# Moving a 64-byte scratch tile: attention's weights at another address beside the pages of h

## The chip, the cores and the metric

The program runs on one core of one Trainium2 chip. The metric is the device time in microseconds, the median of three runs: 2238.1 us (2237.97 to 2238.53). Beside it stands one profiled execution, from which every duration below is taken.

## The reference, cut to what matters

One transformer block over x of 2048 rows by 1024 columns. Six modulation vectors come from a small vector c; then attention with a linear memory, in 32 heads of 32 and 4 segments of 512 rows; then a mixer MLP across the rows.

```python
mod = (_silu(c) @ w_mod).reshape(c.shape[0], 6, 1, -1)
sa, ca, ga, sb, cb, gb = (mod[:, i] for i in range(6))
h = _layernorm(x) * (1 + ca) + sa
q, k, v = h @ wq, h @ wk, h @ wv          # 32 heads, 4 segments of 512
...
p = _softmax(q_s @ k_s.T * scale + mask)
o = g * (phi(q_s) @ M / den) + (1 - g) * (p @ v_s)
M = M + phi(k_s).T @ v_s
...
x = x + ga * (o @ wo)
h = _layernorm(x) * (1 + cb) + sb
x = x + gb * mixer(h, w1, b1, w2, b2)     # gelu MLP over the rows
```

## The kernel before, in words

**Numbers in two parts.** Large products are made in fp32r from operands split in two: a high part, and the rest. `split` (lines 118 to 125) writes both into one tile `[128, 2, 512]`, 4096 bytes in each partition, and each product takes three matmuls: high by high, high by rest, rest by high.

**Pages and weights.** The normed and modulated x, turned over, is `h`. It stays in SBUF in 16 "pages" of 4096 bytes (`new_page`, line 144), one for each segment and each 128 of the 1024 columns. For a group of four heads the projection weights stay in six of eight tiles tagged `w`, also 4096 bytes each (lines 156 to 171): four for k and v, two for q.

**The projections.** For each group (8) and segment (4), `project` calls:

- `kv_chunk` (line 188): the stationary operand, the one that is loaded into TensorE's array, is 128 columns of an h page; the moving operand, the one that streams through it, is 256 columns of a weight tile. This is line 195, output `nps`, 3072 matmuls in all.
- `q_chunk` (line 199): the other way round. The stationary operand is 128 columns of a weight tile, the moving operand a whole half page of h, 512 columns. This is line 203, output `qps`, 768 matmuls.

Every matmul has its own weight load, and all the steps from one operand slice to the next within these tiles are multiples of 512 bytes.

**The order of the work.** The program is written out in one stream. The main loop (line 691) steps through 128 pairs of head group, segment and head; in each step it issues `scores` of a head that comes three steps later in `maxima`, `values` of the head before, a quarter of a later `project`, and a list of extra jobs (`plan`, `later`) that were given a step by hand: token tiles, weight fetches, late modulation. A scheduler then orders each engine's instructions; on TensorE the projections' matmuls and those of scores and values alternate in short runs. After the loop come the output projection with `wo` (line 793, output `po`) and the MLP (line 923, output `mx`).

**Where things lie.** Tiles are given out from pools that stack up from the low end of each partition; each tile's size is rounded up to 32 bytes. From the low end:

- `const`: a few small tiles, among them `sc` and, opened late in the text at line 570, `mcol` (128 bytes);
- `page`: the 16 pages of h;
- `par`: five tiles of 4096 bytes (`scb`, `gaw`, three buffers `raw`);
- `acst`: `pad2` 32 bytes, `bd` 544, `csb` 64, `saca` 64, `MZ` 4224, `bdg` 4224: 9152 bytes in all;
- `paw`: the eight weight tiles `w`;
- above them the first stage's x and later `prj`, `late` and `sk`, with the operands of scores (`sk`, whose queries and keys are halves of one tile), values (`vp`) and memory (`pq`, `pk`, `v32`).

From the high end come `ident`, `mask` and, in the main loop, the softmax's `p32` and `ph`.

**Distance.** Pages and weights are multiples of 4096 apart, but for `acst`. 9152 is 35 times 256 plus 192, so each slice of a weight tile lies 192 bytes above a slice of a page, modulo 256; seen from the weights, the pages lie 64 above. In the output projection the pages hold `wo`, and the other operand `ots` lies above them with only tiles of 4096 and 8192 bytes between: a distance of 0. In the MLP the addresses of `sp` and of `bA`, `bB` and `bU` give 0 too. "Distance" below is always the address of the stationary operand less that of the moving one, modulo 256: 64 for line 195, 192 for line 203, 0 for lines 793 and 923.

**The two small tiles.** `csb` (line 104) takes the vector c at the start; the norms of the first two segments (`norm_all`, line 214, lines 217 to 236) then use its 16 floats as scratch for means, variances and scales. `mcol` takes the 32 sums of late modulation (`mod_late`, line 577), one column each, in the main loop.

Of the kernel before, what the change touches and what calls it, by code (L numbers as in the profile page):

```python
# [7 lines left out]
F32 = mybir.dt.float32  # L8
# [10 lines left out]
P = 128  # L19
NSEG, L = 4, 512  # L20
NK = D // P
# [23 lines left out]
def attention_and_mlp(ctx, tc, x, wq, wkv, wo, beta, w1, b1, w2, b2, c, wm_a, wm_b, out):  # L45
# [15 lines left out]
    const = ctx.enter_context(tc.tile_pool(name="const", bufs=1))  # L61
# [3 lines left out]
    a = par.__enter__()  # L65
    scb, gaw = (a.tile([P, D], F32, name=n) for n in ("scb", "gaw"))
    acst_pool = tc.tile_pool(name="acst", bufs=1)
    acst = acst_pool.__enter__()
# [32 lines left out]
    V.reciprocal(gate[:, 0], gate[:, 1])  # L101
    V.tensor_scalar(gate[:, 1], gate[:, 0], -1.0, 1.0, op0=ALU.mult, op1=ALU.add)

    csb = acst.tile([P, 2, NK], F32, name="csb")
    SY.dma_start(csb[:, 0], c)
    A.activation(csb[:, 1], csb[:, 0], AF.Exp, scale=-1.0)
    V.tensor_scalar_add(csb[:, 1], csb[:, 1], 1.0)
# [429 lines left out]
    def values(t, h):  # L537
# [28 lines left out]
        A.copy(ot, ps)  # L566
        SY.dma_start(oT[g, :, L * seg:L * seg + L], ot)
        del st[t]

    mcol = const.tile([P, 4 * NK], F32, name="mcol")  # L570

    def mod_fetch(j):
        r = a.tile([P, D], F32, tag="raw", bufs=3, name=f"rawm{j}")
# [569 lines left out]
```

## Time and profile before

| what | us |
|---|---|
| median of three runs | 2238.1 |
| the profiled execution | 2237.2 |
| its span | 2235.5 |
| outside the span | 1.7 |
| TensorE busy in the span | 2194.0 |
| VectorE, ScalarE, GpSimd busy | 1678.2, 1136.2, 731.9 |

A profile's row names an engine, a line and the program's tiles (out<-in). PE is TensorE's matmul, PEld its weight load. The mean of a group is the time of one matmul from start to end, pipeline included, so that matmuls overlap. What a matmul costs in a stream is the step from one start to the next, its pace. The view that shows it is the chain of work that ended last: a piece there gives its start, its length and the number of matmuls in a row, and length by number is the pace.

### The profile page before, as it was taken

What the parts mean: (1) busy time and instruction counts of PE and PEld (TensorE: products, weight loads), DVE (VectorE), ACT (ScalarE), POOL (GpSimd) and SP (SyncE); (2) the same over time, 40 slices, a digit from 0 to 9 for tenths busy, and PEclk for the clock granted to TensorE, in tenths of its full rate; (3) what the DMA queues carried; (4) which work ended last, traced back from release to release, by engine and by line L of the source; (5) the groups of instructions that cost most, each with busy time, mean ns of one, the idle gap of its engine ahead of it and who ended that gap; (6) DMA issues with size and microseconds to landing.
All of it is one profiled execution on the core that took longest, in us unless ns stands there. A gap on an engine that the chain in (4) does not pass through costs nothing.

```text
span 2235.5 us, 38277 instructions
## 1 busy us (share of the span) xinstructions
PE 2194.0 (98%) x13786; PEld 1883.5 (84%) x13786; DVE 1678.2 (75%) x3762; ACT 1136.2 (51%) x2082; POOL 731.9 (33%) x831
## 2 busy tenths in 40 slices
PE   8999999998999999999999999999999999999999
PEld 5989898887999899888888888888888888888887
DVE  7677677766777777655758766888888886969687
ACT  5477777665666666655546633533334242424232
POOL 2176666656777676654001200033330000000000
PEclk9999999999999999999999999999999999999999
DMA  7656665687566566665664587655556541414134
GB/s 284 192 175 205 170 180 168 179 299 230 163 194 194 162 197 185 195 192 181 226 205 161 222 328 261 251 212 222 206 201 232 204 144 59 153 57 146 57 123 151
DMA packets 175185, 423.05 MB, mean 189 GB/s; under 512 B 17524, under 2 KB 71828, under 8 KB 166036
## 3 DMA queue, kind: packets, MB, share of 16 engines
q1 hardware_dynamic: 174996, 420.61, 57.2%
q8 instruction: 109, 1.79, 0.3%
q14 instruction: 80, 0.66, 0.1%
HBM read 244.62 MB, written 125.06 MB: 165 GB/s over the span
## 4 chain that ended last, share of the span: by engine, by line
PE 84%; POOL 4%; DMA 3%; ACT 3%; DVE 3%; issue 2%; SPq 1%; ACTq 0%; DVEq 0%; POOLq 0%
PE mx L923 48%; PE nps L195 11%; PE po L793 8%; PE qps L203 6%; PE pv L549 3%; POOL ph L535 2%; PE a L520 1%; PE sz L484 1%; ACT ph L533 1%; DMA sk<-nt 1%; PE sx L484 1%; DVE wv L125 1%; POOL p L531 1%; PE a L523 1%; PE up L466 1%
## 5 line engine op out<-in xcount | busy, mean ns | idle before, releaser
L923 PE MATMUL mx<-bU,sp 128*128 128x512 f32 x2352 | 534.2, 389 | 0.9 <-DVE ac L930 0.9
L923 PEld LDWEIGHTS mx<-bU,sp 128*128 128x128 f32 x2352 | 441.1, 188 | 93.5 <-issue 1.3
L195 PE MATMUL nps<-wv,h 128*128 128x256 f32 x3072 | 437.9, 282 | 1.8 <-POOL h L125 0.7
L535 POOL TENSOR_TENSOR ph<-p,ph 128x640 f16<-128x640 f32 x256 | 383.6, 1520 | 156.1 <-ACT ph L533 153.3
L122 ACT CAST sp<-wr 128x384 fp32r<-128x384 f32 (+2 forms) x408 | 217.0, 545 | 426.7 <-PE mx L923 347.3
L923 PE MATMUL mx<-bA,sp 128*128 128x512 f32 x1764 | 430.5, 389 | 0.0
L195 PEld LDWEIGHTS nps<-wv,h 128*128 128x128 f32 x3072 | 404.6, 189 | 9.9 <-DVE h L125 2.0
L923 PEld LDWEIGHTS mx<-bA,sp 128*128 128x128 f32 x1764 | 331.1, 188 | 68.8
L125 DVE TENSOR_TENSOR sp<-wr,sp 128x384 fp32r<-128x384 f32 (+2 forms) x408 | 260.5, 650 | 31.1 <-ACT sp L122 30.8
L930 DVE TENSOR_TENSOR ac<-mx,ac 128x512 f32<-128x512 f32 x280 | 190.3, 688 | 85.1 <-PE mx L923 84.4
L203 PE MATMUL qps<-h,wq 128*128 128x512 f32 x768 | 198.3, 399 | 0.2
L533 ACT CAST ph<-p 128x1280 f16<-128x1280 f32 x128 | 161.3, 1260 | 44.4 <-POOL p L531 43.7
L793 PE MATMUL po<-wo,ots 128*128 128x512 f32 x768 | 179.3, 390 | 0.0
L793 PEld LDWEIGHTS po<-wo,ots 128*128 128x128 f32 x768 | 143.3, 188 | 29.0 <-DVE x L796 0.2
L923 PE MATMUL mx<-bB,sp 128*128 128x512 f32 x588 | 164.0, 389 | 0.0
L203 PEld LDWEIGHTS qps<-h,wq 128*128 128x128 f32 x768 | 140.7, 189 | 27.5 <-ACT vp L407 0.9
L531 POOL TENSOR_SCALAR_AFFINE_SELECT p<-p 128x256 f32<-128x256 f32 x256 | 121.9, 487 | 99.2 <-ACT p L528 52.4
L549 PE MATMUL pv<-vp,ph 128*128 128x97 bf16 (+1 forms) x2560 | 143.8, 203 | 3.0 <-DVE red L556 1.5
L549 PEld LDWEIGHTS <-ph 128*128 128x128 f16 x2560 | 115.8, 99 | 26.6 <-issue 11.5
L486 DVE CUSTOM_DVE_ANT_0 sx<-sx,mask 128x128 f32<-128x128 f32 (+1 forms) x256 | 93.8, 366 | 49.3 <-PE sx L484 47.4
L923 PEld LDWEIGHTS mx<-bB,sp 128*128 128x128 f32 x588 | 110.3, 188 | 22.9
L930 DVE TENSOR_TENSOR cc<-mx,cc 128x512 f32<-128x512 f32 x140 | 95.0, 685 | 39.6 <-PE mx L923 39.6
(207 smaller groups left out, 3165.7 us busy)
## 6 DMA issues: line engine op xcount, KB each, us to landing
sk<-sg SPq DMA_DIRECT2D x384, 128.0 KB
wr<-in_w_dram SPq DMA_DIRECT2D x28, 1024.0 KB
wr<-in_w_dram SPq DMA_DIRECT2D x32, 768.0 KB
bstu<-ucd SPq DMA_DIRECT2D x28, 768.0 KB
wsp<-wv SPq DMA_DIRECT2D x32, 512.0 KB
rawm<-in_wm_b_dram SPq DMA_DIRECT2D x32, 512.0 KB
wv<-wsp SPq DMA_DIRECT2D x32, 512.0 KB
pcd<-cc SPq DMA_DIRECT2D x14, 1024.0 KB
```

What stands on the lines that cost most here:

```text
L122: last_hi[0] = A.copy(hi, src)
L125: return lo_eng.tensor_tensor(lo, src, hi.bitcast(F32), op=ALU.subtract)
L195: T.matmul(ps[:, aa], h[:, j, 128 * tt:128 * tt + 128], wt[:, i, o:o + 256], start=(n == 0), stop=(n >= 6 * NK - 2), skip_group_check=True)
L203: T.matmul(ps, wt[:, i, o:o + 128], h[:, j], start=(k + n == 0), stop=(3 * k + n == 3 * NK - 1))
L486: marks[4 * t + h - LEADS, "V"] = V.tensor_tensor_reduce(o, o, mask[:, 384 - 128 * i:], 1.0, -3.0e38, op0=ALU.add, op1=ALU.max, accum_out= ...
L531: G.affine_select(w, w, pattern=[[0, 2], [1, 128]], compare_op=ALU.is_ge, fill=0.0, base=0, channel_multiplier=-1)
L533: marks[n, "A"] = A.copy(ph[:, 0], p32)
L535: marks[n, "G"] = G.tensor_tensor(ph[:, 1, c], p32[:, c], ph[:, 0, c], op=ALU.subtract)
L549: T.matmul(pv[:, i, 0:w], ph[:, part, o:o + 128], d["vp"][:, j, h, 0:w], start=(n == 0), stop=(n == 19), skip_group_check=True)
L793: T.matmul(ps, os_[:, i, P * ct:P * ct + P], wop[ct, nh][:, j], start=(n == 0), stop=(n == 3 * NK - 1))
L923: T.matmul(ps, ops[q][:, i, P * k:P * k + P], b[:, j], start=(m == 0 and first), stop=(m == 3 * nk - 1), skip_group_check=True)
L930: V.tensor_tensor(d, ps, d, op=ALU.add)
```

## The change

`mcol` is opened in `const` at the place where `csb` was made, and `csb` becomes a view of `mcol`'s first 16 columns. Nothing else is edited: no instruction is added, removed or changed in shape.

```diff
-    csb = acst.tile([P, 2, NK], F32, name="csb")
+    mcol = const.tile([P, 4 * NK], F32, name="mcol")
+    csb = mcol[:, 0:2 * NK].rearrange("p (a k) -> p a k", a=2)
     SY.dma_start(csb[:, 0], c)
     A.activation(csb[:, 1], csb[:, 0], AF.Exp, scale=-1.0)
     V.tensor_scalar_add(csb[:, 1], csb[:, 1], 1.0)
...
         SY.dma_start(oT[g, :, L * seg:L * seg + L], ot)
         del st[t]
 
-    mcol = const.tile([P, 4 * NK], F32, name="mcol")
-
     def mod_fetch(j):
```

In `const` only the order of the small tiles changes, not their sum, so the pages stay where they were. `acst` shrinks by 64 bytes to 9088, which is 35 times 256 plus 128. What lies above `csb` moves down by 64: `saca`, `MZ`, `bdg`, the weight tiles, and all of `prj`, `late` and `sk`. The distance is then 128 for line 195 and for line 203 alike.

## The prediction

> **What bounds the kernel now.** I read the page first: its span, the busy shares and the chain that ended last.
>
> ```profile
> span 2235.5 us, 38277 instructions
> PE 2194.0 (98%) x13786; PEld 1883.5 (84%) x13786; DVE 1678.2 (75%) x3762; ACT 1136.2 (51%) x2082; POOL 731.9 (33%) x831
> PE mx L923 48%; PE nps L195 11%; PE po L793 8%; PE qps L203 6%; PE pv L549 3%; POOL ph L535 2%; PE a L520 1%; PE sz L484 1%; ACT ph L533 1%; DMA sk<-nt 1%; PE sx L484 1%; DVE wv L125 1%; POOL p L531 1%; PE a L523 1%; PE up L466 1%
> ```
>
> TensorE is busy almost throughout, and four of its lines hold 73% of the chain. The change touches two, lines 195 and 203, 17% together. The view of busy time by windows says where they run: start, attention, output projection, MLP.
>
> ```profile
> 0.00:70.00 70.00, 60.35 (x353) 42.25 (x354) 50.72 (x105) 36.56 (x64) 17.71 (x52) 0.98 0.78 285
> 70.00:968.00 898.00, 870.85 (x7683) 796.92 (x7682) 646.69 (x1895) 592.44 (x1088) 571.65 (x665) 0.99 0.65 192
> 968.00:1160.00 192.00, 191.98 (x1035) 158.81 (x1034) 119.59 (x320) 93.63 (x169) 43.04 (x50) 1.00 0.62 207
> 1160.00:2235.50 1075.50, 1070.87 (x4722) 885.55 (x4720) 861.21 (x1445) 413.55 (x765) 99.51 (x64) 1.00 0.50 178
> ```
>
> The columns are window, length, busy time of PE, PEld, DVE, ACT and POOL, granted clock, DMA share and GB/s. In attention PE is busy 870.85 of 898 us, the next engine (DVE) 646.69; the granted clock is 0.98 to 1.00 everywhere, so a difference in pace between lines is not the clock's. Attention is the stage to read, and in it what one matmul costs.
>
> For that I use the chain in order of time: start, length, count. First the two lines that do not change, whose operands lie at distance 0.
>
> ```profile
> 1051.74 112.25 PE po L793 x495
> 1163.99 36.04 PE mx L923 x159
> ```
>
> 112.25 / 495 = 226.8 ns and 36.04 / 159 = 226.7 ns for 512 moving columns, over hundreds in a row. Half of it, 113.4, is what 256 columns would take at this rate. Now the two lines of the change, at distance 64 (nps, 256 columns) and 192 (qps, 512 columns).
>
> ```profile
> 61.64 8.04 PE nps L195 x68
> 76.87 2.96 PE nps L195 x26
> 199.53 2.50 PE nps L195 x22
> 206.79 2.47 PE nps L195 x21
> 225.61 2.06 PE nps L195 x18
> 477.54 3.53 PE nps L195 x31
> 481.83 3.17 PE nps L195 x27
> 500.67 2.52 PE nps L195 x22
> 710.79 2.29 PE nps L195 x20
> 187.09 5.51 PE qps L203 x24
> 727.65 4.83 PE qps L203 x21
> ```
>
> nps has two paces. Runs such as x26 (113.8), x22 at 199.53 (113.6) and x31 (113.9) sit on the floor of 113.4; others such as x68 (118.2), x21 (117.6) and x27 (117.4) are 4 ns above it. Over the nine rows it is 29.54 us / 255 = 115.8 ns. qps is on its floor in neither row: 10.34 / 45 = 229.8 ns against 226.8. The durations say the same of all matmuls (minimum, median, maximum of each line):
>
> ```profile
> L195 PE MATMUL nps<-wv,h x3072: 276/279/507, 26.4 to 958.6; 128*128 128x256 f32 x192
> L203 PE MATMUL qps<-h,wq x768: 387/393/689, 27.0 to 967.3; 128*128 128x512 f32 x192
> L793 PE MATMUL po<-wo,ots x768: 387/389/481, 968.3 to 1163.6; 128*128 128x512 f32 x192
> ```
>
> qps and po have the same shape and the same three products, yet their medians are 393 and 389 ns. So there is something to gain, and it is small: two lines, a few ns each.
>
> **The change part by part.** *The move of csb.* Its instructions stay. The question is a wait: `mod_late` will write into columns that the norms have read.
>
> ```profile
> L236 ACT ACTIVATE x<-x,csb x4: 1227/1258/1291, 18.0 to 49.5; 128x1024 f32<-128x1024 f32 x4
> L578 DVE SCALAR_TENSOR_TENSOR rawm<-rawm,scb x32: 1208/1624/2402, 397.9 to 862.6; 128x1024 f32<-128x1024 f32 x32
> ```
>
> The last reader of csb starts at 49.5 us and takes 1.3; the first writer of mcol starts at 397.9. A wait, if one is written, has been over for 347 us. It costs nothing; were the cover gone, what is queued on DVE behind `mod_late` would be the maxima of the next heads. No DMA is added or passed.
>
> *The distance of lines 195 and 203.* This is the whole sum. No matmul of these shapes at distance 128 is in the trace, so the cost is bounded from both sides.
>
> - Upper gain: both reach the floor of po and mx. nps: 3072 x (115.8 - 113.4) = 7.4 us. qps: 768 x (229.8 - 226.8) = 2.3 us. Together 9.7 us.
> - Upper loss: nps always at the pace of its slowest quoted run: 3072 x (118.2 - 115.8) = 7.4 us; qps as much above its pace as it is above the floor, 2.3 us. Together 9.7 us again, though nothing excludes a pace that this trace does not contain.
>
> Not all of it reaches the end. In attention PE's lines share the chain with other engines, as the chain of that window shows:
>
> ```profile
> by line: PE nps L195 24.4%; PE qps L203 15.7%; PE pv L549 6.6%; POOL ph L535 5.3%; issue 3.8%; ACT ph L533 2.5%; PE a L520 2.4%; PE sz L484 2.3%; DMA sk<-nt 2.3%; PE sx L484 2.1%; POOL p L531 1.9%; PE up L466 1.8%; DMA sk<-sg 1.7%; DMA rawm
> 70.00:968.00 898.00, 410.62 (x2880) 380.02 (x2880) 0.99 0.65 192
> 70.00:968.00 898.00, 189.90 (x744) 136.66 (x744) 0.99 0.65 192
> ```
>
> The last two rows are the same window for line 195 and line 203 alone. The chain holds 40.1% of 898 = 360 us of their 600.5 us busy: 0.60 would be the least that comes through. PE's busy share of the window, 0.97, is the most. I take 0.8, because PE works in order and a shorter projection also brings scores and values forward; what is late next is POOL's and ACT's work on `ph`, 7.8% of that chain. That leaves 5.8 to 9.4 us, and 7.8 us at 0.8.
>
> Which end? The three distances with rows are 0 (only the floor), 64 (both paces) and 192 (never the floor). The distances with stalls are the two odd multiples of 64. After the change the weights lie at the pages' place modulo 128, as the operands of po and mx do. If what collides repeats every 128 bytes, 128 is as good as 0. If it repeats every 256, 128 lies between 64, which is half good, and 192, which is bad. I take the first, narrowly: it needs no third behaviour beyond those in the rows.
>
> Here the Trainium skill speaks against the change. "SBUF — State Buffer", Who interferes with whom, gives TensorE two read ports of its own, one for each operand, and says that it never waits on anyone; an address would then be no matter at all. The trace doesn't bear it out for po and qps, 226.8 against 229.8 ns, though it doesn't prove the address to be the reason. By the page the sum would be 0; it is a rival below.
>
> *The other tiles that moved.* Scores, values, memory and the transposes lose or gain 64 bytes against h, `ph` and `ident`. Within scores and memory both operands move. The transposes of three tiles show whether their distance mattered:
>
> ```profile
> L247 PE MATMUL hps<-ident,x x64: 270/273/477, 24.0 to 58.6; 128*128 128x128 f32 x64
> L564 PE MATMUL ops<-ident,am x128: 270/273/421, 128.0 to 1051.5; 128*128 128x128 f32 x128
> L416 PE MATMUL kps<-ident,k x128: 270/273/455, 47.8 to 960.1; 128*128 128x128 f32 x128
> ```
>
> Their distances are 96 and 224 (hps), 0 (ops) and 96 (kps), and all three medians are 273: nothing. Where a run of scores meets a projection, some 500 times, the distance goes from 0 to 64; at the 2 ns by which nps now stands above its floor that is 1 us, at most 2 with the 4 ns of its upper pace, either way. I take 0 and keep 1 in the range.
>
> **Sum.** The profiled execution took 2237.2 us, 1.7 outside its span, and the median is 0.9 above it. 2238.1 - 7.8 = 2230.3; the likeliest case spans 2228 to 2233.
>
> **Rivals.**
>
> - *The address is not the reason.* Nothing moves: 2238, within 3 us. For it: nps shows both paces at one distance, so a run's start matters too; and attention runs beside more work of ACT and POOL than po does. Against it: qps is off the floor in every run quoted, po and mx in none.
> - *Slower: distance 128 is the middle of a period of 256.* nps then keeps its upper pace, 118.2, and qps loses as much again: 9.7 us at 0.8 is 7.8 us, giving 2246. It decides as soon as more than about half of nps's runs sit on the upper pace; a half is about where it stands. For it: going round from 64 (half) to 192 (none) passes 128. Against it: 0 and 128 differ from both by the same amounts.
> - *Half and half.* One of the two lines gains and the other loses, or only qps reaches the floor: 2.3 x 0.8 = 1.8 us, 2236.
> - *The instructions are ordered anew*, since the scheduler sees one tile where there were two. The shapes and durations are the same, so I see no reason; a few us either way, and it does not stand alone.
>
> **How the numbers follow.** Floor 0.43 (2230.3), nothing 0.20 (2238), half and half 0.12 (2236), slower 0.25 (2246). The bound of what can be told from no change is 0.2%, 4.5 us: 2233.6 and 2242.6. Of the floor case nearly all lies below it, of the slower one most above: faster 0.43, same 0.33, slower 0.24. The range takes in the floor case with its full 9.4 us and a little of the joints, and the slower one: 2228 to 2247.
>
> **What would show it.** Right: qps's median at 389 and its mean at 390 as po has; nps's median at 276 or 277; runs of nps at 113.4 only, of qps at 226.8; attention's window shorter by 6 to 9 us, output projection and MLP unchanged. Wrong: nps's median at 281 or more, or runs above 118; or both medians unchanged, which is the first rival. A shift in po's or mx's stage would mean that something else moved.

## The result, and the profile after

The changed kernel takes 2241.36 us (median of 16 runs) against 2237.6 for the kernel before (16 runs): a ratio of 1.0018, 95% interval 1.0011 to 1.0025, so 4.0 us slower, between 2.5 and 5.6. The prediction had 2230.3 as the likeliest time and 2246 for the case in which distance 128 is a bad one.

The order and the shapes of all instructions are the same in both programs, engine by engine. In the profiled executions the span grew from 2235.5 to 2238.3 us. The view of busy time by windows, for attention up to the first matmul of the output projection, and for the output projection alone, first of the kernel before, then of the kernel after (window, length, busy time of PE, PEld, DVE, ACT, POOL, granted clock, DMA share, GB/s):

```profile
70.00:968.30 898.30, 871.15 (x7685) 797.22 (x7684) 646.99 (x1895) 592.74 (x1088) 571.95 (x666) 0.99 0.65 192
968.30:1163.80 195.50, 195.48 (x1048) 161.68 (x1048) 119.29 (x320) 97.13 (x176) 42.75 (x50) 1.00 0.61 204
```

```profile
70.00:971.20 901.20, 878.65 (x7687) 804.54 (x7687) 648.65 (x1895) 593.32 (x1088) 571.21 (x666) 0.99 0.64 191
971.20:1166.70 195.50, 195.48 (x1048) 161.65 (x1048) 119.09 (x320) 97.17 (x176) 42.77 (x50) 1.00 0.62 205
```

All of the difference lies in attention, which is 2.9 us longer. The output projection is 195.50 us in both, and what follows it 1071.7 us before and 1071.6 after (span less the window's end). Inside attention PE is busy 7.5 us longer (878.65 less 871.15), but stands idle 4.6 us less: 901.20 - 878.65 = 22.55 us, against 27.15 before. That difference is where a part of the loss went; it is taken up again below. The granted clock doesn't explain the 2.9 us: by the clock's records it stood at half for 17.1 us of attention in both profiled executions (two stretches of 6.8 and one of 3.4).

The chain in order of time of the kernel after shows which matmuls are slower. These are the same runs of matmuls as in the prediction's fence (line numbers are larger by one in this kernel up to 570, smaller by one behind it):

```profile
200.74 2.60 PE nps L196 x22
207.99 2.49 PE nps L196 x21
226.91 2.17 PE nps L196 x18
481.31 3.68 PE nps L196 x31
485.76 3.28 PE nps L196 x27
188.36 5.57 PE qps L204 x24
730.27 4.88 PE qps L204 x21
1054.62 112.25 PE po L792 x495
```

nps: x22 went from 113.6 to 118.2 ns a matmul, x31 from 113.9 to 118.7, x18 from 114.4 to 120.6, x27 from 117.4 to 121.5, x21, slow already, from 117.6 to 118.6. None of these is left on the floor of 113.4. qps: 10.45 us / 45 = 232.2 ns, against 229.8. po, which the change doesn't reach, still takes 226.8. The durations (minimum, median, maximum) say it for all of them:

```profile
L196 PE MATMUL nps<-wv,h x3072: 274/281/390, 26.6 to 961.4; 128*128 128x256 f32 x192
L204 PE MATMUL qps<-h,wq x768: 387/393/632, 27.2 to 970.2; 128*128 128x512 f32 x192
L792 PE MATMUL po<-wo,ots x768: 387/389/483, 971.2 to 1166.5; 128*128 128x512 f32 x192
```

The median of nps rose from 279 to 281, the value named beforehand as the sign of being wrong; that of qps stayed at 393, though its pace rose. So the pace, from start to start, is the better view.

From here on "mean step" is the mean time from the start of a matmul to the next of the same line, from the trace's starts, without steps that wait on a semaphore and without those over 130 ns (line 195) or 250 ns (line 203). It is 116.1 ns before and 118.9 after for line 195, 229.9 and 232.5 for line 203.

### The profile page after: what moved, and what is told of

Same layout as the page of the kernel before. It is cut to its first block, busy times and chain, and to the rows that moved or that the text cites. A ratio compares the mean times of both kernels' runs of the same rounds, so it can differ in the third digit from the quotient of the medians.

```text
span 2238.3 us, 38277 instructions
## 1 busy us (share of the span) xinstructions
PE 2200.3 (98%) x13786; PEld 1890.3 (84%) x13786; DVE 1681.0 (75%) x3762; ACT 1137.2 (51%) x2082; POOL 729.2 (33%) x831
## 4 chain that ended last, share of the span: by engine, by line
PE 87%; POOL 3%; DVE 3%; DMA 2%; ACT 2%; issue 2%; SPq 1%; ACTq 0%; DVEq 0%; POOLq 0%
PE mx L922 47%; PE nps L196 12%; PE po L792 8%; PE qps L204 8%; PE pv L550 3%; POOL ph L536 2%; PE a L521 1%; PE sz L485 1%; PE sx L485 1%; ACT ph L534 1%; PE a L524 1%; PE sy L485 1%; PE srow L298 1%; PE up L467 1%; PE rd L457 1%
## 5 line engine op out<-in xcount | busy, mean ns | idle before, releaser
L196 PE MATMUL nps<-wv,h 128*128 128x256 f32 x3072 | 445.4, 285 | 1.2 <-DVE h L126 0.5
L196 PEld LDWEIGHTS nps<-wv,h 128*128 128x128 f32 x3072 | 410.1, 189 | 8.7 <-DVE h L126 1.9
```

The costliest lines, as they stand in the source:

```text
L196: T.matmul(ps[:, aa], h[:, j, 128 * tt:128 * tt + 128], wt[:, i, o:o + 256], start=(n == 0), stop=(n >= 6 * NK - 2), skip_group_check=True)
```

## The experiments

The theory after the result: **the distance of the two operands modulo 256 sets the pace of a stream of matmuls**, and each shape has distances of its own that suit it. The rivals: moving csb costs something itself; the tiles above the weights pay; or the weights' own address counts, whatever the other operand's. All times below are medians, the ratio is to runs of the kernel before on the same chip.

### The move of csb without the addresses, and the addresses without the move

`e1_csb_alone` is the changed kernel with 64 bytes given back below the weights:

```diff
-    acst.tile([P, 8], F32, name="pad2")
+    acst.tile([P, 24], F32, name="pad2")
```

> csb lies in mcol's place as in the change, but pad2 is 64 bytes larger, so that every tile above lies where it lay before (distances 64 and 192). Address theory: the kernel before, within 0.1% (2237 us), medians of 279 ns for line 195's matmul and 393 for line 203's, as before. Rival, that moving csb itself costs: as slow as the change, 2241 us.

`e2_pad_to_128` is the kernel before, with `csb` in its old tile:

```diff
-    acst.tile([P, 8], F32, name="pad2")
+    acst.tile([P, 56], F32, name="pad2")
```

> The kernel before with pad2 larger by 192 bytes: csb stays in its own tile, and all tiles above it lie at the change's places modulo 256 (distance 128 for both lines). Address theory: the change's time, 2241 us, ratio 1.0018, and its runs: nps at 119 ns a matmul, qps at 232. Rival, that moving csb costs: the kernel before, 2237 us. A third outcome, that the exact address counts and not only its rest modulo 256, would show other paces than the change's.

e1: 2237.58 us, ratio 1.0002 (0.9993 to 1.0010). e2: 2241.31 us, ratio 1.0019 (1.0010 to 1.0028). Mean steps of e1: 116.1 and 230.2 ns; of e2: 118.9 and 232.4. Moving csb costs nothing that can be measured, and the addresses alone cost what the change costs. In e2 the weights lie 192 bytes higher than before, in the change 64 lower: 256 apart, and to the tenth of a nanosecond the same mean step of line 195.

### The weights, or the tiles above them

`e5_above_alone` puts 192 bytes behind the weight tiles; `e6_weights_alone` puts 192 below them (`pad2` of 56) and 64 behind:

```diff
+    behind_w = tc.tile_pool(name="bw", bufs=1)
+    behind_w.__enter__().tile([P, 48], F32, name="pad3")     # e6: 16
...
```

> 192 bytes of padding behind the weight tiles: weights and pages keep their distances (64 and 192), the tiles above (scores, values, memory) move by the change's 64 bytes modulo 256. Theory, that only the distance of weights and pages counts: as before, within 0.1%, nps and qps at their paces of before. Rival, that the tiles above pay for the change, where a run of scores meets a projection: about 2241 us.

> 192 bytes of padding below the weight tiles and 64 behind them: the weights are at the change's distance of 128, the tiles above where they were modulo 256. Theory, that only the distance of weights and pages counts: the change's 2241 us, nps at 119 ns and qps at 232. Rival, the tiles above: as before, 2237 us.

e5: 2235.87 us, ratio 1.0000 (0.9992 to 1.0009). e6: 2241.06 us, ratio 1.0017 (1.0009 to 1.0026), mean steps 118.6 and 232.5. The tiles of scores, values and memory don't matter; the weights alone make the change's loss.

### Distance 0, and the distances swapped

`e3_distance_0` and `e4_swapped` are the kernel before with `pad2` of 24 and of 40:

> The kernel before with pad2 larger by 64 bytes: distance 0 for both lines, as the output projection and the MLP have. Address theory: nps at 113.4 ns and qps at 226.8 after the first few matmuls of a run; 9 us of matmul time less than before, 0.6 to 1.0 of it in the end: 2228 to 2232 us. Rival, that attention's own traffic and not the distance keeps these lines off the floor: 2238 us, paces as before.

> The kernel before with pad2 larger by 128 bytes: the distances of the two lines change places, 192 for line 195 and 64 for line 203. Address theory with a period of 256: line 195 at 192 has no floor any more, some 117 to 119 ns; line 203 at 64 gains its floor in part of the runs, 227 to 230; together 2236 to 2243 us. If the stalls repeat every 128 bytes in distance, both lines are as before, 2238 us; but then the change, at 128, would have been on the floor.

e3: 2241.22 us, ratio 1.0020 (1.0011 to 1.0029), where I expected 2228 to 2232. e4: 2240.38 us, ratio 1.0012 (1.0003 to 1.0021). The chain of e3, the same runs:

```profile
201.47 2.62 PE nps L195 x22
485.45 3.71 PE nps L195 x31
489.93 3.31 PE nps L195 x27
188.97 5.47 PE qps L203 x24
733.41 4.79 PE qps L203 x21
```

qps did what was expected: 10.26 / 45 = 228.0 ns, and within a run it settles at 226.7 after three to eleven matmuls (22 runs of 14 or more, at full clock); its median duration fell to 389 ns, as po has. nps did the contrary: 119.1, 119.7 and 122.6 ns, the slowest so far, on the very distance at which 512 columns come down to their floor. So the floor of one line says nothing about another line at the same distance. e4 is the other half: line 195 at 192 has 118.1, as expected, and line 203 at 64 has 233.3, where 227 to 230 was expected. The two lines want different distances, and swapping them spoils both.

### All eight places, 32 bytes apart

`e9` to `e12` move the weights alone (padding below, and behind them what is missing to 256):

```diff
-    acst.tile([P, 8], F32, name="pad2")
+    acst.tile([P, 16], F32, name="pad2")     # e10: 64, e11: 48, e12: 32
...
+    behind_w.__enter__().tile([P, 56], F32, name="pad3")     # e10: 8, e11: 24, e12: 40
...
```

> Weights alone moved, by 32 bytes: distance 32 for line 195, 224 for line 203; the tiles above stay where they were modulo 256. If pace is smooth in the distance, between its neighbours: line 195 between 119.5 (at 0) and 116.1 (at 64), 117.8 ns; line 203 between 229.5 (at 0) and 230 (at 192). Matmul time 5 us more than before, of which the runs so far passed 0.4 to the end: 2238 to 2239 us. If it is not smooth, any pace; below 116 would be a better place than any so far.

> Weights alone, distance 96 for line 195 and 160 for line 203. Smooth: 117.5 ns (between 116.1 and 118.9) and 231 ns (between 232.4 and 230); 5 us more matmul time, at 0.4 passed on: 2238 to 2239 us. Not smooth: any pace.

> Weights alone, distance 160 for line 195 and 96 for line 203. Smooth: 118.5 ns (between 118.9 and 118.1) and 233 ns (between 233.3 and 232.4); 9.6 us more matmul time, at 0.4 passed on: 2240 us. Not smooth: any pace.

> Weights alone, distance 224 for line 195 and 32 for line 203. Smooth: 118.8 ns (between 118.1 and 119.5) and 231 ns (between 229.5 and 233.3); 9.3 us more matmul time, at 0.4 passed on: 2240 us. Not smooth: any pace.

Times: e9 2239.96 us, ratio 1.0013 (1.0005 to 1.0022); e10 2241.45, 1.0019 (1.0010 to 1.0027); e11 2242.94, 1.0028 (1.0017 to 1.0039); e12 2238.82, 1.0014 (1.0005 to 1.0023). The mean steps by distance, with the kernel that each is from:

| distance | line 195, 256 columns | line 203, 512 columns |
|---|---|---|
| 0 | 119.5 (e3) | 229.5 (e3) |
| 32 | 118.5 (e9) | 233.2 (e12) |
| 64 | 116.1 (before) | 233.3 (e4) |
| 96 | 118.6 (e10) | 233.9 (e11) |
| 128 | 118.9 (after) | 232.5 (after) |
| 160 | 119.4 (e11) | 233.5 (e10) |
| 192 | 118.1 (e4) | 229.9 (before) |
| 224 | 117.6 (e12) | 233.1 (e9) |

The curves are not smooth: line 203 goes from 229.5 at 0 to 233 at 32 to either side. Line 195 has one distance that stands out, 64; line 203 has two, 0 and 192. The kernel before had line 195 at its best and line 203 at its second best, and each of the seven shifts of all the weights together, in steps of 32, lost time.

### Both lines at their best

`e7_q_at_0` gives the q weights tiles of their own, 64 bytes up, and leaves the k and v weights where they were; `e8_split_control` has the same two tags with paddings of 256, so the old distances:

```diff
+    aq.tile([P, 16], F32, name="padq")       # e8: 64
...
-            w = aw.tile([P, 2, 512], F32R, tag="w", bufs=8, ...)
+            w = (aw if kind == "v" else aq).tile([P, 2, 512], F32R, tag="w", bufs=6 if kind == "v" else 2, ...)
...
```

> Two tags instead of one: six weight tiles for k and v at the old place (distance 64 for line 195), two for q at distance 0 for line 203. Theory, that each line has a distance of its own: line 195 as before (116 ns, two paces), line 203 on the floor of 226.8 after its first matmuls. Against the control with the same tags and q at 192: 768 x 3 ns = 2.3 us less matmul time, 1.4 to 2.3 us in the end.

> The control of the kernel before it: the same two tags, both at the old distances (64 and 192). Whatever the fewer spare tiles for q cost shows here alone: 2236 to 2242 us. Paces of lines 195 and 203 as in the kernel before.

e7: 2237.97 us, ratio 1.0006 (0.9997 to 1.0016). e8: 2236.48 us, ratio 1.0003 (0.9994 to 1.0012). The step of line 203 is 229.0 ns in e7 and 230.2 in e8, line 195 the same (116.2, 116.3). The floor is reached, but the first matmuls of every run stand above it, and the runs are short (24 at most): 768 x 1.2 = 0.9 us, not the 2.3 us that I had taken. No difference in time can be told, so no version tried here beats the kernel before.

### Distance, or the weights' own address; and another stage

In all runs so far the pages stood still. `e13_both_moved` and `e14_pages_moved` move them; `e15_mlp_192` lets the MLP's tiles move along:

```diff
-    st = const.tile([P, 2, 6], F32, tag="st", bufs=4, name="st")      # both places
+    st = const.tile([P, 2, 6], F32, tag="st", bufs=3, name="st")
...
+    sp.tile([P, 16], F32, name="pad4")                                # not in e15
...
-    acst.tile([P, 8], F32, name="pad2")
+    acst.tile([P, 24], F32, name="pad2")                              # e14 only
```

> Three buffers instead of four for the norms' statistics take 64 bytes out of const, so that pages and weights both lie 64 bytes lower (64 bytes of padding put the MLP's tiles back): the weights lie where the change has them, at distances 64 and 192 as before. Theory, that the distance counts: line 195 at 116 ns, line 203 at 230, time as before within 0.1%. Rival, that the weights' own address counts: the change's paces, 119 and 232 ns, and 2241 us.

> The same, and 64 bytes of padding below the weights: the weights lie where they lay before the change, the pages 64 bytes lower, distance 0 for both lines. Theory, that the distance counts: line 195 at 119.5 ns, line 203 on its floor of 227 after some matmuls, 2241 us as with the weights moved to distance 0. Rival, that the weights' own address counts: as before, 116 and 230 ns, 2237 us.

> As the first of these three, but without the padding that puts the MLP's tiles back: the MLP's stationary tiles lie at distance 192 from bA and bU, and 0 from bB. Theory, that it is a matter of two operands and not of attention: the matmuls with bU leave 226.7 ns for about 230, as line 203 has at 192; 2352 of them and part of those with bA, so 7 to 15 us of matmul time more in a stage where TensorE waits for next to nothing: 2243 to 2252 us. Rival, that it needs attention's company: the MLP's stage as before, 2237 us.

e13: 2236.02 us, ratio 1.0001 (0.9992 to 1.0010), mean steps 116.1 and 230.1: the weights at the change's address modulo 256, and nothing lost. e14: 2240.61 us, ratio 1.0017 (1.0007 to 1.0027), 119.5 and 229.3: the weights at their old address, and the paces of distance 0. The chain of e14:

```profile
202.96 2.63 PE nps L195 x22
484.50 3.71 PE nps L195 x31
488.98 3.31 PE nps L195 x27
190.53 5.49 PE qps L203 x24
```

Within 0.02 us these are e3's, in which the weights were moved and not the pages. It is the distance.

e15: 2251.91 us, ratio 1.0071 (1.0058 to 1.0085), 15.9 us slower. The chain of the MLP's stage, first before, then e15:

```profile
1163.99 1065.28 PE mx L923 x4698
```

```profile
1159.94 1078.57 PE mx L923 x4685
```

1065.28 / 4698 = 226.8 ns became 1078.57 / 4685 = 230.2. Over 4704 matmuls that is 16.0 us of matmul time, and the kernel lost 15.9 by the ratio (14.9 between the medians): in a stage where PE waits for next to nothing, all of it or nearly all comes through.

The mean hides three paces, and the expectation missed one of them. The matmuls with bU, at distance 192, go round 226, 229, 232 ns in long runs, just as line 203 does at 192. Those with bA, at 192 too, take 231.4, and those with bB 232.5 (means of the steps from one to the next of the same operand), though bB moved along with the stationary tiles and is still at distance 0. The durations show it as well, first before, then e15:

```profile
L923 PE MATMUL mx<-bU,sp x2352: 387/389/499, 1691.5 to 2231.4; 128*128 128x512 f32 x196
L923 PE MATMUL mx<-bB,sp x588: 389/389/389, 1165.9 to 1704.7; 128*128 128x512 f32 x196
```

```profile
L923 PE MATMUL mx<-bU,sp x2352: 388/392/469, 1695.7 to 2240.6; 128*128 128x512 f32 x196
L923 PE MATMUL mx<-bB,sp x588: 387/393/401, 1158.8 to 1709.1; 128*128 128x512 f32 x196
```

bB comes in threes between nines of bA, and in e3 a run at distance 0 needed three to eleven matmuls to settle. So a matmul's own distance doesn't fix its step alone; that short runs don't settle would explain it, but no run here separates that from other causes.

The Trainium skill's "SBUF — State Buffer", Who interferes with whom, would have all this at nothing, since it gives TensorE two read ports and says that it never waits on anyone. The runs here don't agree: moving one of the two operands changed the pace by up to 3% (116.1 to 119.5 ns for line 195).

## Why the prediction was wrong, step by step

- **csb's move and its wait:** right. It was costed at nothing, and e1 has 1.0002.
- **The two lines are the place, and nothing else moves:** right. e5 and e6 tell it apart, the output projection and the MLP are unchanged.
- **The tiles above, 0 with 1 us either way:** right (e5, 1.0000). The three equal medians that it was argued from could not have shown it, though: qps's median didn't move either when its pace did.
- **"Which end?": the failed step.** I took it that "what collides repeats every 128 bytes", so that 128 would be as good as 0, and counted nps's gain down to 113.4 from it. Two things in it fell. The paces don't repeat every 128 (qps has 232.5 at 128 and 229.5 at 0), but they do every 256 (after and e2 agree). And distance 0 isn't good for line 195: its floor there was carried over from po and mx, while for line 195 it is the worst of the eight places, 119.5. Even a period of 128 would thus have brought no gain. The rows had hinted at it: line 195's best runs, on the floor, were at 64, not at 0.
- **The rival "slower, 128 is the middle of a period of 256":** its sign was right, and its sum of matmul time, 9.7 us, nearly too: 3072 x 2.8 = 8.6 and 768 x 2.6 = 2.0, so 10.6 us. Its picture of going round from good to bad was not: line 203's places 32 bytes apart don't lie between their neighbours.
- **"I take 0.8": wrong by half.** Of 10.6 us came 4.0, a share of 0.38, below the 0.60 that I had held for the least. Worked out in the same way for all ten kernels that move both lines to other distances, the share is 0.30 to 0.47. The windows show where a part went: PE's idle time in attention fell by 4.6 us. It is not chance: in the six profiles with both lines at the old distances (before, e1, e5, e8, e13, e15) it is 24.1 to 27.2 us, in the three at 128 (after, e2, e6) 19.4 to 22.5. Most likely what scores and values wait for arrives in its own time, whatever the projection takes. The waits of PE in attention, before and then after:

```profile
PE sx L484 <- DMA sk<-sg: 8.1, 2, 6.8
PE a L520 <- DMA sk<-nt: 4.3, 5, 1.7
PE sz L484 <- DVE mx L486: 4.0, 5, 1.3
```

```profile
PE sx L485 <- DMA sk<-sg: 6.9, 3, 5.3
PE sz L485 <- DVE mx L487: 4.4, 5, 1.5
PE a L521 <- DMA sk<-nt: 2.7, 2, 1.9
```

The waits for the DMAs that stack the scores' operands fell from 12.4 to 9.6 us. PE was busy only 7.5 us longer, not 10.6. By the trace's starts, counted from the same matmul to the first po, the steps without idle time in them grew by 9.6 us, but the steps with some went from 50 to 42, and what these hold besides idle time (the matmul ahead running to its end, some 0.3 us a step) went from 15.6 to 13.1 us. So fewer waits gave back more than their idle time. A share of the chain is no share that a loss passes on: the chain says who was last, not how soon the next would have been.
- **The bounds of the unknown cost:** the loss, 10.6 us of matmul time, lies just beyond the bound of 9.7, and nps alone beyond its own (8.6 for 7.4). The measured time lies inside the range, but the range takes in the gain and the loss alike, so that says little for the mechanism.

## What to carry to other kernels

Where the two operands of a dense stream of matmuls come from different tiles, their distance modulo 256 was worth up to 3% of the stream's pace here (fp32r, a weight load for each matmul), so look at the step from start to start against a stream of the same shape whose operands lie elsewhere. A good distance for one line is not one for another, and the places between must be measured, not interpolated. Lines 195 and 203 differ in the number of moving columns, but also in which tile is stationary and in how often a slice is streamed again; which of these makes the difference was not tried. That 512 columns settle at 226.7 ns at distance 0 and go round 226, 229, 232 at 192 was seen on three lines (po, mx, qps) and on two (mx, qps). In attention, a stage with waits, less than half of the loss came through (0.30 to 0.47); in the MLP, all or nearly all.

## What the runs showed of the hardware that was not expected

- The pace of a stream settles into a pattern of its own. At distance 192 the steps of line 203 go round 226, 229, 232 ns; at 128 mostly round 228, 230, 233, 241, 232, 231, 232; at 0 they start between 224 and 240 and then stay at 227. At 192 the pattern isn't tied to the place in the run: among runs of 16 and more the 226 stands in each of the three places. Line 195 at 64 has two paces, 113.3 and 117.7. Behind a matmul of sx all eleven runs of ten and more settle at the first, behind sz or a some at each; what decides was not tried.
- The granted clock drops to half for 3.4, 6.8 or 10.2 us, two to five times in attention, in every profiled execution. One stretch in both kernels follows the longest wait (6.8 us before, 5.3 after); others follow only short ones. The windows of the kernel after, ahead of such a stretch and in it:

```profile
460.00:464.60 4.60, 2.75 (x30) 2.23 (x30) 4.07 (x14) 3.88 (x8) 3.60 (x5) 1.00 0.97 327
464.60:468.00 3.40, 3.40 (x10) 2.67 (x9) 3.40 (x7) 2.05 (x3) 3.31 (x3) 0.50 1.02 416
```

PE was busy 2.75 of 4.60 us, its longest wait there 1.50 us, and then seven steps of qps in a row took 426 or 427 ns each. In seven of the kernels such a stretch stands some 125 us in, behind waits of 0.6 us at most; what brings it on was not tried. Over all the profiles the clock stands at half for 10.2 to 27.3 us of attention, so single executions can differ by more than the change does; the ratios above rest on 6 to 16 runs.
